# Packing the gate and up turns into one PSUM bank and one copy, and fusing two coefficient multiplies, in a fused state-space and ReGLU backward kernel

## The chip, the cores and the metric

One core of a Trainium2 chip. The metric is the device time of one execution in microseconds (us).

The engines are called PE (TensorE, matmuls and transposes), ACT (ScalarE), DVE (VectorE), POOL (GpSimd) and SP (SyncE, issues DMAs). PSUM is where PE writes; ACT and DVE move ("evict") its results into SBUF.

## The reference

The forward pass is a layernorm whose result feeds two branches that are added to the input: a state-space convolution (done by FFT) and a feed-forward block. The kernel computes the output and the gradients of all inputs.

```python
gate = x @ W_gate;  up = x @ W_up           # x: 2048 x 576, weights 576 x 4608
gate = gate * (gate > 0)
h    = gate * up
y    = h @ W_down                           # 4608 x 576
# convolution branch: K[d,l] = Re sum_n C[d,n] exp(l*dt*A[d,n]) dt*B[d,n],  y_A = fft_conv(u, K) + u*Dskip
# out = x0 + y_A(xn) + y_B(xn);  then jax.vjp: gradients of 12 inputs
```

## The kernel before

The feed-forward block runs in 12 chunks of 384 hidden columns. For each chunk, each of its three tiles of 128 columns and each of four groups of 512 rows (144 units in all), a unit computes gate, up and the gradient of h (15 matmuls of 128x512), makes three tiles T (h, and the gradients of gate and up), and *turns* them: PE transposes each into PSUM, and an engine copies the result into hN, dgN or duN, which the weight gradients of the chunk read later. The convolution's work (named S4 in the code, tiles ps_s) is woven in between by generators.

```python
def copy(self, out, in_, cols, scale=None, fp32=True):      # class Balance: who evicts?
    cd = cols * (1.09e-3 if fp32 else 0.56e-3) + 0.06       # account of DVE
    ca = cols * 0.84e-3 + 0.06                              # account of ACT
    if self.d + cd <= self.a + ca:  ...  # DVE copies
    else:                           ...  # ACT copies

# a_unit, for gate, up and dh in turn:
    for k in range(NK):
        nc.tensor.matmul(ps[:], lhsT=w[:, k, fs], rhs=rhs[:, k, :], ...)
    for _ in turns:
        next(src)                                           # one turn: 4 transposes, one copy

def t_steps(self, units):
    for c, sg, ft in units:
        for src, dst in zip(self.T[(c, sg, ft)], (self.hN, self.dgN, self.duN)):
            pt = g.psum_mm.tile([P, 512], F32, name="ps_mm")[:].bitcast(BF16)...   # 5 buffers of a bank
            for j in range(JS):                                                    # JS = 4
                nc.tensor.transpose(out=pt[:, j, :], in_=src[:, j * P:(j + 1) * P], ...)
            g.bal.copy(dst[...], pt[:, 0:JS, :], 512, fp32=False)                  # half a bank
            yield

# p2, generation of the convolution kernel, 36 groups of 16 channels:
    v.tensor_tensor(xa[:], pw[:, 1, hs]..., self.ev[:]..., op=ALU.mult)            # starts a group
    ...                                                                            # cut
    v.tensor_tensor(X[:, :, 0:2, :], Wv..., ex..., op=ALU.mult)
    nc.scalar.activation(X[:, :, 2, :], X[:, :, 0, :], ACT.Copy, scale=-1.0)
    v.tensor_tensor(w1, pw[:, 2, hs]..., X[:, :, 1:3, :]..., op=ALU.mult)          # w1 lies in tile xa
    v.tensor_tensor(w2, pw[:, 3, hs]..., X[:, :, 0:2, :]..., op=ALU.mult)          # w2 lies in tile W
    v.tensor_tensor(XC[:]..., w1, w2, op=ALU.subtract)
    ...                                  # cut: Y, V by group of 4; matmuls; sums(): V = X * psum, reduced
```

## Time and profile before

| | before |
|---|---|
| median of the first three runs | 1794.33 us |
| PE / DVE / ACT busy | 96% / 74% / 66% |
| PE starts later than its own spacing (gaps over 60 ns, at full clock) | 103 us |
| the same, lost at half clock | 10 us |

The first two lines are from the page: the span, and each engine's busy time, its share and its instructions.

```profile
span 1792.3 us, 42070 instructions
...
PE 1719.7 (96%) x16449; PEld 1184.7 (66%) x16449; DVE 1317.8 (74%) x2867; ACT 1189.2 (66%) x2736; POOL 205.0 (11%) x246
```

The next lines are the view of stretches (from:to in us, its length, busy us and instructions of PE, weight loads, DVE, ACT, POOL, then granted clock, DMA share and GB/s).

```profile
core 0: us, PE busy (x) PEld busy (x) DVE busy (x) ACT busy (x) POOL busy (x), PEclk, DMA share, GB/s
...
100.00:290.00 190.00, 170.70 (x1358) 109.97 (x1357) 139.38 (x322) 133.40 (x326) 16.02 (x21) 0.97 0.96 306
290.00:1490.00 1200.00, 1174.09 (x11904) 818.03 (x11903) 961.86 (x1956) 817.11 (x1838) 160.23 (x168) 1.00 0.70 183
```

In the long middle stretch PE is busy 98% of the time, DVE 80% and ACT 68%.

The last two rows of the table are not on the page. I take the start of each matmul and of the next: in this trace matmuls that follow each other stand 216 ns apart for 512 columns, 162 for 384, 122 for 288, 62 for 144 and 56 for 128 (medians), which N/2.4 + 2.5 ns for N columns fits, and 25 ns for 16 and 32. What a pair has beyond that is PE's wait. The view of groups, ACT only, shows the evictions (line, engine, op, tiles, sizes, count | busy us, mean ns of one | idle us before them and what ended it):

```profile
L68 ACT CAST osx<-ps_mm 128x288 bf16<-128x288 f32 x682 | 260.5, 428 | 50.5 <-PE ps_mm L298 47.6
...
L68 ACT COPY dgN<-ps_mm 128x512 bf16<-128x512 bf16 x140 | 83.8, 599 | 17.3 <-PE ps_mm L270 16.3
L68 ACT CAST dhb<-ps_mm 128x512 bf16<-128x512 f32 x141 | 83.8, 594 | 49.6 <-PE ps_mm L244 47.7 <-DVE dhb L221 0.8
L68 ACT COPY duN<-ps_mm 128x512 bf16<-128x512 bf16 x135 | 81.9, 607 | 1.5 <-PE ps_mm L270 1.1
L68 ACT COPY hN<-ps_mm 128x512 bf16<-128x512 bf16 x137 | 81.6, 595 | 1.2 <-PE ps_mm L270 1.2
```

The turn copies cost about 0.60 us each. The two multiplies, DVE's groups:

```profile
L867 DVE TENSOR_TENSOR xa<-pw,X 128x512 f32<-128x512 f32 x36 | 24.5, 681 | 0.1
L868 DVE TENSOR_TENSOR W<-pw,X 128x512 f32<-128x512 f32 x36 | 24.5, 681 | 0.0
```

### The profile page before, as it was taken

To read this page: it belongs to the slowest core of one execution; us is meant where nothing else is said; L and a number is where in the kernel's file an instruction comes from. 1 tells how busy PE (TensorE), PEld (TensorE's weight loads), DVE (VectorE), ACT (ScalarE), POOL (GpSimd) and SP (SyncE) were. 2 spreads that over 40 slices of the span, in tenths; PEclk is the share of its full clock that TensorE was granted. 3 is DMA by queue.
4 is the path that set the end of the run, shared out by engine and by line. 5 is a ranking of instruction groups with operands and counts; after the bars stand their busy time and mean duration, and the time that the engine had idled before them with its cause. 6 is when DMAs were issued, how large, how long until landed. Compare 5 with 4: busy or idle time off the path is not lost.

```text
span 1792.3 us, 42070 instructions
## 1 busy us (share of the span) xinstructions
PE 1719.7 (96%) x16449; PEld 1184.7 (66%) x16449; DVE 1317.8 (74%) x2867; ACT 1189.2 (66%) x2736; POOL 205.0 (11%) x246
## 2 busy tenths in 40 slices
PE   7989989999999999999999999999999998999998
PEld 5665557667667666766766766766676675676776
DVE  7575884677789788678787889889978962972551
ACT  5875874786688477568468658747857845864651
POOL 0200112011022011012101101101111100110000
PEclk9999999999999999999999999999999999999999
DMA  9799989679568656766858856866766578995873
GB/s 297 265 332 303 331 233 295 194 182 253 165 145 228 192 139 157 226 183 147 229 154 190 230 156 142 212 188 151 181 185 152 112 212 257 260 288 157 270 240 100
DMA packets 239004, 373.30 MB, mean 208 GB/s; under 512 B 49491, under 2 KB 153429, under 8 KB 237269
## 3 DMA queue, kind: packets, MB, share of 16 engines
q1 hardware_dynamic: 212836, 304.09, 52.4%
q0 software_dynamic: 24384, 51.92, 18.6%
q10 hardware_dynamic: 1584, 14.60, 2.3%
q8 instruction: 129, 2.11, 0.5%
q14 instruction: 71, 0.57, 0.1%
HBM read 233.10 MB, written 137.43 MB: 207 GB/s over the span
## 4 chain that ended last, share of the span: by engine, by line
PE 63%; DVE 21%; ACT 7%; DMA 6%; issue 3%; SPq 1%; POOL 0%; ACTq 0%; DVEq 0%; POOLq 0%
PE ps_mm L298 17%; PE ps_mm L244 15%; PE ps_mm L352 11%; PE ps_mm L336 6%; PE ps_mm L270 3%; DVE V L935 2%; DVE T L261 2%; DVE Sm L936 2%; DVE V L881 1%; DVE Y L882 1%; DVE Y L880 1%; DVE rg L254 1%; PE ps_mm L370 1%; DMA gT<-in_gT_dram 1%; DVE X L861 1%
## 5 line engine op out<-in xcount | busy, mean ns | idle before, releaser
L298 PE MATMUL ps_mm<-wf,T 128*128 128x288 bf16 x3456 | 481.8, 287 | 7.4 <-DVE T L256 2.6
L298 PEld LDWEIGHTS <-T 128*128 128x128 bf16 x3456 | 324.5, 98 | 97.0 <-issue 12.9
L68 ACT CAST osx<-ps_mm 128x288 bf16<-128x288 f32 x682 | 260.5, 428 | 50.5 <-PE ps_mm L298 47.6
L311 POOL DMA_DIRECT2D acc_dram<-osx x160 | 138.8, 867 | 1027.8 <-ACT osx L68 590.7
L352 PEld LDWEIGHTS <-rows 128*128 128x128 bf16 x1536 | 146.2, 98 | 95.4 <-issue 1.6
L244 PE MATMUL ps_mm<-xT,wd_150 128*128 128x512 bf16 x720 | 181.1, 379 | 4.1 <-ACT xT L153 1.6
L270 PEld LDWEIGHTS <-T 128*128 128x128 bf16 x1728 | 127.5, 98 | 86.3 <-issue 4.7
L244 PE MATMUL ps_mm<-xT,wd_151 128*128 128x512 bf16 x720 | 180.8, 380 | 0.0
L254 DVE SCALAR_TENSOR_TENSOR rg<-rg,ps_mm 128x512 bf16<-128x512 bf16 x144 | 98.2, 682 | 108.3 <-PE ps_mm L244 68.6
L244 PE MATMUL ps_mm<-gT,wd_152 128*128 128x512 bf16 x705 | 175.9, 379 | 0.7 <-DMA gT<-in_gT_dram 0.7
L270 PE MATMUL ps_mm<-ident_bf,T 128*128 128x128 bf16 x1728 | 157.6, 220 | 4.8 <-DVE T L256 1.9
L336 PE MATMUL ps_mm<-rows,hN 128*128 128x144 bf16 x2304 | 158.9, 227 | 0.0
L336 PEld LDWEIGHTS <-hN 128*128 128x128 bf16 x2304 | 148.5, 98 | 8.0 <-issue 5.4
L68 ACT CAST obw<-ps_mm 128x384 bf16<-128x384 f32 x103 | 49.2, 478 | 144.7 <-PE ps_mm L352 112.4
L352 PE MATMUL ps_mm<-dgN,rows 128*128 128x384 bf16 x768 | 136.8, 326 | 0.5 <-DMA rows<-xs_dram_141 0.5
L352 PE MATMUL ps_mm<-duN,rows 128*128 128x384 bf16 x768 | 135.6, 326 | 0.0
L253 ACT ACTIVATE rg<-ps_mm 128x512 bf16<-128x512 f32 x144 | 86.9, 603 | 52.1 <-PE ps_mm L244 51.5
L68 ACT CAST dhb<-ps_mm 128x512 bf16<-128x512 f32 x141 | 83.8, 594 | 49.6 <-PE ps_mm L244 47.7
L261 DVE TENSOR_TENSOR T<-dhb,rg 128x1024 bf16<-128x1024 bf16 x141 | 101.0, 717 | 19.4 <-ACT dhb L68 18.7
L244 PEld LDWEIGHTS <-wd_150 128*128 128x128 bf16 x720 | 66.0, 97 | 61.5 <-issue 3.7
L244 PEld LDWEIGHTS <-wd_151 128*128 128x128 bf16 x720 | 65.4, 98 | 59.9 <-issue 3.3
L244 PEld LDWEIGHTS <-wd_152 128*128 128x128 bf16 x705 | 63.4, 98 | 58.8 <-issue 1.8
(2506 smaller groups left out, 3042.2 us busy)
## 6 DMA issues: line engine op xcount, KB each, us to landing
acc_dram<-osx POOLq DMA_DIRECT2D x176, 288.0 KB, 5.1
gT<-in_gT_dram SPq DMA_DIRECT2D x48, 640.0 KB, 6.2
xT<-xT_dram SPq DMA_DIRECT2D x44, 640.0 KB, 5.8
rows<-in_gq_dram SPq DMA_DIRECT2D x48, 576.0 KB, 4.3
wf<-in_Wf_dram ACTq DMA_DIRECT2D x11, 1296.0 KB, 8.9
ex_dram<-exs SPq DMA_DIRECT2D x36, 320.0 KB, 4.6
ex<-ex_dram SPq DMA_DIRECT2D x36, 320.0 KB, 4.5
out_dram<-obw SPq DMA_DIRECT2D x96, 96.0 KB, 2.7
```

What stands on the lines that cost most here:

```text
L68: self.nc.scalar.copy(out, in_)
L244: nc.tensor.matmul(ps[:], lhsT=w[:, k, fs], rhs=rhs[:, k, :], start=(k == 0), stop=(k == NK - 1))
L253: nc.scalar.activation(rg, ps_g[:], ACT.Relu)
L254: nc.vector.scalar_tensor_tensor(upm, rg, 0.0, ps_u[:], op0=ALU.is_gt, op1=ALU.mult)
L261: nc.vector.tensor_tensor(T[:, 1:3], dhb.unsqueeze(1).to_broadcast([P, 2, JS * P]), ru[:], op=ALU.mult)
L270: nc.tensor.transpose(out=pt[:, j, :], in_=src[:, j * P:(j + 1) * P], identity=g.ident_bf[:])
L298: nc.tensor.matmul(ps[:, cs], lhsT=lt, rhs=rh, start=(i == 0), stop=(i == len(mms) - 1))
L311: nc.gpsimd.dma_start(g.acc_dram[:, t, :, :], o[:], accum_op=ALU.add)
L336: nc.tensor.matmul(ps[:, ft * 144:(ft + 1) * 144], lhsT=self.hN[:, st, ft * P:(ft + 1) * P], rhs=gq[:, st, :], start=(st == 0), stop=(st = ...
L352: nc.tensor.matmul(ps[:, :Fc], lhsT=xs[:, st, 0:P], rhs=src[:, st, :], start=(st == 0), stop=(st == ST - 1))
L935: nc.vector.tensor_tensor(pr[:, vi], X[:, dx:dx + DG, r0:r0 + 2].rearrange("p d r a -> p d (r a)").unsqueeze(2).to_broadcast(sh), psg[:, 0 ...
L936: nc.vector.tensor_reduce(out=Sm[:, :, s0 + dd:s0 + dd + DG, :].rearrange("p v d j -> p v (d j)"), in_=pr.rearrange("p v d j c -> p v (d j ...
```

## The change

Intent: fewer fixed costs on ACT and DVE, and fewer PSUM tiles. The turns of the two gradients share a bank, eight transposes of 128x128 bf16, and leave it in one copy of 1024 columns; the two multiplies become one over both planes (which needs the planes of `pw` swapped, and an input that reads overlapping windows of X).

```diff
-        self.dgN = wp.tile([P, ST, Fc], BF16, name="dgN")
-        self.duN = wp.tile([P, ST, Fc], BF16, name="duN")
+        self.gN = wp.tile([P, 2, ST, Fc], BF16, name="gN")
+        self.dgN, self.duN = self.gN[:, 0], self.gN[:, 1]
 ...                                                            # a_unit: 2 turns per unit, behind up and dh
-            for _ in turns:
+            n = (2 * len(turns) * (i + 1)) // 3 - (2 * len(turns) * i) // 3
+            for _ in range(n):
                 next(src)
 ...                                                            # t_steps
-            for src, dst in zip(self.T[(c, sg, ft)], (self.hN, self.dgN, self.duN)):
+            for which in ((0,), (1, 2)):
+                n = len(which) * JS
                 pt = g.psum_mm.tile([P, 512], F32, name="ps_mm")...
-                    nc.tensor.transpose(out=pt[:, j, :], in_=src[:, j * P:(j + 1) * P], ...)
-                g.bal.copy(dst[...], pt[:, 0:JS, :], 512, fp32=False)
+                for i, w in enumerate(which):
+                    for j in range(JS):
+                        nc.tensor.transpose(out=pt[:, i * JS + j, :], in_=src[w][:, j * P:(j + 1) * P], ...)
+                if n == JS:
+                    g.bal.copy(self.hN[:, js, fs], pt[:, 0:n, :], n * P, fp32=False)
+                else:
+                    g.bal.copy(self.gN[:, :, js, fs], pt[:, 0:n, :].rearrange(...), n * P, fp32=False)
 ...                                                            # p2
-                w1 = xp.tile(xs, F32, name="xa")...
-                w2 = xp.tile([P, 2, SX, NE], F32, name="W")...
-                v.tensor_tensor(w1, pw[:, 2, hs]..., X[:, :, 1:3, :]..., op=ALU.mult)
-                v.tensor_tensor(w2, pw[:, 3, hs]..., X[:, :, 0:2, :]..., op=ALU.mult)
-                v.tensor_tensor(XC[:]..., w1, w2, op=ALU.subtract)
+                w = xp.tile([P, 2, SX, NE], F32, name="W")...
+                xv = bass.AP(x.tensor, x.offset, [x.ap[0], (16, 2)] + list(x.ap[1:]))
+                v.tensor_tensor(w, pw[:, 2:4, hs]..., xv, op=ALU.mult)
+                v.tensor_tensor(XC[:]..., w[:, 1], w[:, 0], op=ALU.subtract)
```

More of the change, by code (lines that the diff above doesn't have):

```diff
@@ L245, in a_unit @@
             pss.append(ps)
-            for _ in turns:
+            n = (2 * len(turns) * (i + 1)) // 3 - (2 * len(turns) * i) // 3
+            for _ in range(n):
                 next(src)
-            yield NK * 0.2158 + len(turns) * 0.22
+            yield NK * 0.2158 + n * 0.33
         ps_g, ps_u = pss[0:2]
@@ L266, in t_steps @@
         for c, sg, ft in units:
-            for src, dst in zip(self.T[(c, sg, ft)], (self.hN, self.dgN, self.duN)):
+            src, js, fs = self.T[(c, sg, ft)], slice(sg * JS, (sg + 1) * JS), slice(ft * P, (ft + 1) * P)
+            for which in ((0,), (1, 2)):
+                n = len(which) * JS
                 pt = g.psum_mm.tile([P, 512], F32, name="ps_mm")[:].bitcast(BF16).rearrange("p (k t) -> p k t", t=P)
-                for j in range(JS):
-                    nc.tensor.transpose(out=pt[:, j, :], in_=src[:, j * P:(j + 1) * P], identity=g.ident_bf[:])
-                g.bal.copy(dst[:, sg * JS:(sg + 1) * JS, ft * P:(ft + 1) * P], pt[:, 0:JS, :], 512, fp32=False)
+                for i, w in enumerate(which):
+                    for j in range(JS):
+                        nc.tensor.transpose(out=pt[:, i * JS + j, :], in_=src[w][:, j * P:(j + 1) * P], identity=g.ident_bf[:])
+                if n == JS:
+                    g.bal.copy(self.hN[:, js, fs], pt[:, 0:n, :], n * P, fp32=False)
+                else:
+                    g.bal.copy(self.gN[:, :, js, fs], pt[:, 0:n, :].rearrange("p (i j) t -> p i j t", i=2), n * P, fp32=False)
                 yield
@@ L599, in params @@
                 v.tensor_tensor(p1[:], p1[:], p2[:], op=op)
-                v.tensor_tensor(pw[:, 2 + j, :], p1[:], dt[:], op=ALU.mult)
+                v.tensor_tensor(pw[:, 3 - j, :], p1[:], dt[:], op=ALU.mult)
                 bal.add(d=2.6)
@@ L863, in p2 @@
                 XC = xop.tile([P, SX, 2, 16], BF16, name="XC")
-                xw = [P, SX, 32]
-                w1 = xp.tile(xs, F32, name="xa")[:].rearrange("p d e -> p (d e)")[:, 0:SX * 32].rearrange("p (d e) -> p d e", e=32)
-                w2 = xp.tile([P, 2, SX, NE], F32, name="W")[:].rearrange("p r d e -> p (r d e)")[:, 0:SX * 32].rearrange("p (d e) -> p d e", e=32)
-                v.tensor_tensor(w1, pw[:, 2, hs].unsqueeze(2).to_broadcast(xw), X[:, :, 1:3, :].rearrange("p d r a -> p d (r a)"), op=ALU.mult)
-                v.tensor_tensor(w2, pw[:, 3, hs].unsqueeze(2).to_broadcast(xw), X[:, :, 0:2, :].rearrange("p d r a -> p d (r a)"), op=ALU.mult)
-                v.tensor_tensor(XC[:].rearrange("p d r a -> p d (r a)"), w1, w2, op=ALU.subtract)
+                xw = [P, 2, SX, 32]
+                w = xp.tile([P, 2, SX, NE], F32, name="W")[:].rearrange("p r d e -> p (r d e)")[:, 0:2 * SX * 32].rearrange("p (w d e) -> p w d e", w=2, e=32)
+                x = X[:, :, 0:2, :].rearrange("p d r a -> p d (r a)")
+                xv = bass.AP(x.tensor, x.offset, [x.ap[0], (16, 2)] + list(x.ap[1:]))
+                v.tensor_tensor(w, pw[:, 2:4, hs].unsqueeze(3).to_broadcast(xw), xv, op=ALU.mult)
+                v.tensor_tensor(XC[:].rearrange("p d r a -> p d (r a)"), w[:, 1], w[:, 0], op=ALU.subtract)
                 bal.add(d=6.5, a=2.5)
@@ L952, in param_grads @@
         S_r, S_i, T_r, T_i = Sm[:, 0, :, 0], Sm[:, 1, :, 0], Sm[:, 0, :, 1], Sm[:, 1, :, 1]
-        pA, pB, cr, ci = (pw[:, i, hs] for i in range(4))
+        pA, pB, ci, cr = (pw[:, i, hs] for i in range(4))
         ob = lambda: yop.tile([P, DG, 2, P], BF16, name="Y")[:].rearrange("p d r q -> p (d r q)")[:, 0:DH]
```

## The prediction

> **What bounds the kernel now.** TensorE. The page's busy table gives PE 1719.7 us of 1792.3 (96%), VectorE (DVE) 1317.8 (74%), ScalarE (ACT) 1189.2 (66%). The timeline shows that PE runs at its own spacing nearly all the time: ten 128x512 matmuls take 2.16 us, eighteen 128x288 take 2.21, sixteen 128x384 take 2.60. From consecutive matmul starts I count about 100 us in which PE issued later than that spacing (gaps over 60 ns), plus about 10 us lost in five stretches at half the clock (granted clock 0.97 in 100-290 us). The Trainium skill, "TensorE: Matmul & The Clock Gate", Part 1, says that an idle window of about 3.4 us halves the clock; the trace agrees: after a 2.4 us wait near 643 us 128x512 matmuls stand 0.43 us apart instead of 0.216. Of the 100 us, about 30 follow an ACT result and 25 a DVE result; others are start-up, DMA round trips or unknown.
>
> **What the change does.** (a) The matmuls and the transposes keep their number and, as the instruction orders of the two builds show, almost exactly their order. PE's own floor doesn't move. (b) 432 evictions of 128x512 bf16 become 144 of 128x512 and 144 of 128x1024; the build gives 136 of the large ones to ACT, 8 to DVE (before: ACT 412, DVE 20). By the group table an ACT copy of 512 takes 0.600 us, one of 1024 (YT, same shape) 1.02, so the busy sum of ACT falls by about 25 us. But instructions overlap: back to back, starts are 0.477 us apart for 512 and 0.909 for 1024, so ACT's queue really gains only 2 x 0.477 - 0.909 = 0.045 us a pair, about 6.5 us in all. The skill, "ScalarE: Activation LUTs", says the same (a fixed term of 186 ns, of which about 93 ns overlap). (c) Two 128x512 fp32 multiplies (0.681 us each, 0.602 apart) become one of 1024; estimate 1.21 us, 1.135 apart: 36 x 0.07 = 2.5 us of DVE queue, about 5 us of its busy sum. (d) A unit takes two turn tiles in place of three from the five-buffer PSUM pool, so reuse is less tight; against that a bank stays closed for 0.9 us in place of 0.48, and evictions behind the long copy wait up to 0.4 us longer.
>
> **How much is on the critical path.** The chain of waits is 63% PE, 21% DVE, 7% ACT. Relief of 1-2% in ACT's queue and 0.3% in DVE's shortens only those of PE's waits that are an eviction late: about 50 us of waits, of which I expect 3 to 8 us to go, and the long copies to give 1 to 3 back. Order changes on ACT and DVE add some chance of either sign, above all whether one of the half-clock stretches appears or goes.
>
> **Prediction.** 1789 us (before 1794.33), range 1779 to 1799 (8 in 10). Chances: faster by over 2% 0.02, within 2% 0.97, slower 0.01.
>
> **What would show it.** ACT busy about 1165 us, DVE about 1310, PE unchanged within 6 us; 144 copies into gN of about 1.03 us on ACT; the multiply about 1.2 us x36; waits of PE that follow ACT somewhat smaller; DMA unchanged.
>
> **What would make it wrong.** If PSUM reuse (d) was the real cause of many small PE waits, the gain could reach 15-20 us. If the long copies hold up the convolution's evictions, or the multiply's overlapping read is slow (over 1.5 us), it could be slower by 5-10 us.

The trace does not quite agree with the idle window of 3.4 us that the prediction takes from the skill: the clock records of the kernel before show half clock from 643.8 us, after a single wait of 2.26 us (2.4 us by the starts of the matmuls), and none after two other waits of 2.26 us (to 239.6 and 272.4 us); the half-clock stretch at 715.5 us follows three waits of 0.76, 0.59 and 0.26 us. The measured stretches decide. And the gain of 0.045 us a pair is the measured one alone, not the skill's (see the last section).

## More of the kernel before

The order in which DVE and ACT get their instructions is not that of the source: it is settled when the program is built, and the traces show it.

From 100 to 290 us the DMA engines are busy 96%, and PE 90%.

## The result, and the profile after

| | before | after |
|---|---|---|
| median, runs of the same rounds | 1794.96 us (4 runs) | 1798.58 us (4 runs) |
| ratio | | 1.0015, 95% interval 0.9997 to 1.0032 |
| the same in five further rounds | 1795.29 us (11 runs) | 1798.06 us (6 runs) |
| ratio there | | 1.0016, interval 1.0001 to 1.0031 |

Ratios are the mean time of one kernel's runs over that of the other's of the same rounds, so not quite the ratio of the medians. The change won nothing, and the second set places it just on the slow side, by some 3 us.

The page of the kernel after, then its stretches (same columns as above):

```profile
span 1797.1 us, 41897 instructions
...
PE 1719.4 (96%) x16449; PEld 1183.1 (66%) x16449; DVE 1313.0 (73%) x2821; ACT 1176.0 (65%) x2602; POOL 204.2 (11%) x246
```

```profile
100.00:290.00 190.00, 168.66 (x1303) 106.73 (x1301) 138.71 (x317) 131.70 (x313) 15.07 (x20) 0.96 0.94 298
290.00:1490.00 1200.00, 1171.35 (x11936) 817.79 (x11934) 958.16 (x1920) 806.58 (x1741) 160.40 (x169) 1.00 0.70 183
```

PE's busy time is unchanged to 0.3 us. ACT gave up 13 us and DVE 5, as intended, and PE did not use them. The evictions and the one multiply after:

```profile
L68 ACT CAST osx<-ps_mm 128x288 bf16<-128x288 f32 x681 | 256.0, 435 | 47.4 <-PE ps_mm L305 45.7
L68 ACT COPY gN<-ps_mm 128x1024 bf16<-128x1024 bf16 x136 | 140.1, 1030 | 8.8 <-PE ps_mm L274 8.5
...
L68 ACT COPY hN<-ps_mm 128x512 bf16<-128x512 bf16 x141 | 83.6, 593 | 26.1 <-PE ps_mm L274 26.0
L68 ACT CAST dhb<-ps_mm 128x512 bf16<-128x512 f32 x141 | 83.4, 591 | 51.2 <-PE ps_mm L244 48.0 <-DVE dhb L221 1.3
```

```profile
L875 DVE TENSOR_TENSOR W<-pw,X 128x1024 f32<-128x1024 f32 x36 | 43.8, 1217 | 0.0
```

Each operation came out as costed: 1.030 us for a copy of 1024, 1.217 us for the multiply. Of the ACT time saved, part became idle time: before its turn copies (hN and gN) ACT now sits idle 34.9 us in all, nearly all of it waiting for PE's transposes (20.0 us before hN, dgN and duN in the kernel before). The Trainium skill, "ScalarE: Activation LUTs", § What ACT_TABLE_LOAD costs, gives 186 ns + 0.833 ns a column for an ACTIVATE with immediate scale and bias. An estimate from that for 512 and 1024 columns is 612 and 1039 ns, and the copies of this trace agree (593 to 607 and 1030 ns).

**Where the time lies.** PE executes the feed-forward matmuls in the same order in both programs (10,337 of them without the turns' transposes), so the k-th matmul of one trace can be set against the k-th of the other. The lag of this matmul, in us, read where the kernel before stands at the time given:

| lag against the one trace of before, us | at 145 | at 290 | at 1490 | at 1785 |
|---|---|---|---|---|
| after | 2.5 | 3.7 | 4.7 | 4.9 |
| after, a second trace | 0.8 | 0.7 | 2.0 | 1.0 |

From 290 us on, where most of the changed instructions are, the change is worth +1.2 or +0.3 us: nothing. The two traces of one kernel differ by 4 us, most of it collected before 290 us. So a systematic difference, if any, is of the size of what one execution differs from the next.

**PE's waits by what ended them** (same counting as in the table of before; us):

| | after an ACT result | after a DVE result | of these, the V product beyond 290 us | all |
|---|---|---|---|---|
| before | 36.4 | 27.6 | 5.3 | 103.4 |
| after | 33.3 | 36.0 | 8.7 | 109.6 |
| after, second trace | 31.1 | 34.5 | 8.7 | 105.2 |

The waits for ACT did shrink by 3 to 5 us. Those for DVE grew by 7 to 8. Two places show how. The timelines below have start us, us, engine, line, op, tiles and sizes, and in brackets the idle time before it and its releaser.

*First place, near 135 us.* Before:

```profile
133.24 0.82 DVE L585 TENSOR_TENSOR exs<-pw,ev 128x640 f32<-128x640 f32 x1 [5.89 <-DMA ex_dram<-exs]
...
134.50 0.45 DVE L62 CAST fA_2069<-ps_s_2070 128x288 bf16<-128x288 f32 x1
...
134.87 0.45 DVE L62 CAST fA_2069<-ps_s_2096 128x288 bf16<-128x288 f32 x1
135.00 0.28 PE L628 MATMUL ps_s_2099<-sig,Sx 128*128 128x288 bf16 x1 [3.15 <-DVE fA_2069 L62]
```

and after:

```profile
137.82 0.82 DVE L592 TENSOR_TENSOR exs<-pw,ev 128x640 f32<-128x640 f32 x1 [6.54 <-DMA ex_dram<-exs]
138.56 0.45 DVE L62 CAST fA_2098<-ps_s_2102 128x288 bf16<-128x288 f32 x1
...
138.93 0.45 DVE L62 CAST fA_2098<-ps_s_2122 128x288 bf16<-128x288 f32 x1
139.06 0.40 PE L635 MATMUL ps_s_2130<-sig,Sx 128*128 128x288 bf16 x1 [5.67 <-DVE fA_2098 L62]
```

In both, DVE stands at a multiply that needs an `exs` buffer whose store has not landed. Evictions of finished matmuls (fA) stand behind it in DVE's queue, and PE runs out of PSUM buffers. The Trainium skill, "TensorE: Matmul & The Clock Gate", Part 1, calls the queues of ACT and DVE strict FIFO; that is what is seen. PE waits 3.15 us before and 5.67 us after: DVE was released by the store at 133.2 us in one and at 137.8 us in the other. By the traces' clock records PE ran at half clock around the end of this wait, for 3.4 us before and for 6.8 us after (in the second trace of the change for 3.4 us, with a wait of 5.3 us).

*Second place, near 1140 us.* Before:

```profile
1140.59 0.69 DVE L859 TENSOR_TENSOR B<-W,ex 128x512 bf16<-128x512 f32 x1
...
1141.19 0.74 DVE L935 TENSOR_TENSOR V<-X,ps_s_18919 128x256 f32<-128x256 f32 x2
...
1141.99 0.62 PE L917 MATMUL ps_s_18963<-ident_bf,Y 128*128 128x128 bf16 x8 [0.31 <-DVE V L935]
```

and after:

```profile
1143.43 0.69 DVE L866 TENSOR_TENSOR B<-W,ex 128x512 bf16<-128x512 f32 x1
...
1144.04 0.82 DVE L851 TENSOR_TENSOR xa<-pw,ev 128x640 f32<-128x640 f32 x1
1144.77 0.74 DVE L942 TENSOR_TENSOR V<-X,ps_s_18678 128x256 f32<-128x256 f32 x2
...
1145.57 0.62 PE L924 MATMUL ps_s_18716<-ident_bf,Y 128*128 128x128 bf16 x8 [1.77 <-DVE V L942]
```

Here V, the product that frees the PSUM buffer PE wants, has the first multiply of the *next* group (`xa`, 0.82 us) in front of it in DVE's order. Before, the V product came directly behind B. PE's wait grew from 0.31 to 1.77 us. In the traces, the next of the ops xa, V, Y and XC behind this `xa` is such a V product 22 times of 36 before and 27 times after.

### The profile page after: what moved, and what is told of

Same layout as the page of the kernel before. It is cut to its first block, busy times and chain, and to the rows that moved or that the text cites. A ratio compares the mean times of both kernels' runs of the same rounds, so it can differ in the third digit from the quotient of the medians.

```text
span 1797.1 us, 41897 instructions
## 1 busy us (share of the span) xinstructions
PE 1719.4 (96%) x16449; PEld 1183.1 (66%) x16449; DVE 1313.0 (73%) x2821; ACT 1176.0 (65%) x2602; POOL 204.2 (11%) x246
## 5 line engine op out<-in xcount | busy, mean ns | idle before, releaser
L305 PEld LDWEIGHTS <-T 128*128 128x128 bf16 x3456 | 324.5, 98 | 100.3 <-issue 16.7
L68 ACT CAST osx<-ps_mm 128x288 bf16<-128x288 f32 x681 | 256.0, 435 | 47.4 <-PE ps_mm L305 45.7
L359 PE MATMUL ps_mm<-gN,rows 128*128 128x384 bf16 x1536 | 265.2, 326 | 0.0
L274 PEld LDWEIGHTS <-T 128*128 128x128 bf16 x1728 | 119.5, 98 | 58.5 <-DVE T L262 0.7
L68 ACT COPY gN<-ps_mm 128x1024 bf16<-128x1024 bf16 x136 | 140.1, 1030 | 8.8 <-PE ps_mm L274 8.5
L274 PE MATMUL ps_mm<-ident_bf,T 128*128 128x128 bf16 x1728 | 141.1, 220 | 0.3 <-DVE T L262 0.2
```

The costliest lines, as they stand in the source:

```text
L68: self.nc.scalar.copy(out, in_)
L274: nc.tensor.transpose(out=pt[:, i * JS + j, :], in_=src[w][:, j * P:(j + 1) * P], identity=g.ident_bf[:])
L305: nc.tensor.matmul(ps[:, cs], lhsT=lt, rhs=rh, start=(i == 0), stop=(i == len(mms) - 1))
L359: nc.tensor.matmul(ps[:, :Fc], lhsT=xs[:, st, 0:P], rhs=src[:, st, :], start=(st == 0), stop=(st == ST - 1))
```

## The experiments

Twelve runs, all with five rounds; each row is against the runs of before. Kernels are compared only within the same rounds. Every interval lies within 1% of 1. "Lag" is that of the table above, from each run's single trace, and has the 4 us of scatter seen there; the three calls also ran on three different chips.

| run | median, us | ratio to before (95%) | lag at 145 / 290 / 1490 / 1785 us |
|---|---|---|---|
| after_again | 1798.06 | 1.0016 (1.0001 to 1.0031) | 0.8 / 0.7 / 2.0 / 1.0 |
| only_turns | 1801.49 | 1.0041 (1.0026 to 1.0055) | 3.2 / 5.0 / 8.2 / 7.5 |
| only_multiply | 1797.62 | 1.0015 (0.9994 to 1.0035) | 0.9 / 2.2 / 6.4 / 5.9 |
| pair_in_two_copies | 1795.83 | 1.0007 (0.9991 to 1.0022) | -1.0 / 0.2 / 4.4 / 6.1 |
| before_act_only | 1801.81 | 1.0033 (1.0021 to 1.0045) | -1.0 / 8.4 / 7.8 / 9.0 |
| after_act_only | 1799.26 | 1.0028 (1.0015 to 1.0042) | 0.0 / 2.7 / 4.6 / 5.1 |
| thin_turns (wrong result) | 1795.06 | 0.9997 (0.9985 to 1.0009) | -0.4 / 4.4 / 3.1 / 2.7 |
| no_multiply (wrong result) | 1801.92 | 1.0033 (1.0021 to 1.0045) | 1.3 / 0.3 / 4.9 / 4.7 |
| before_late_act_only | 1794.28 | 0.9995 (0.9981 to 1.0008) | -3.1 / 4.1 / 4.4 / 3.7 |
| after_late_act_only | 1800.72 | 1.0023 (1.0008 to 1.0038) | -4.8 / 2.9 / 6.2 / 6.8 |
| before_negate_on_dve | 1798.07 | 1.0018 (1.0001 to 1.0035) | -0.8 / 2.3 / 6.4 / 5.3 |
| after_negate_on_dve | 1806.82 | 1.0063 (1.0051 to 1.0075) | 2.8 / 5.3 / 12.8 / 14.3 |

### The change and its parts

after_again is the change unaltered. only_turns keeps the two multiplies, only_multiply keeps the three turn copies. pair_in_two_copies is the change with

```diff
-                    g.bal.copy(self.gN[:, :, js, fs], pt[:, 0:n, :].rearrange(...), n * P, fp32=False)
+                    for i in range(2):
+                        g.bal.copy(self.gN[:, i, js, fs], pt[:, i * JS:(i + 1) * JS, :], JS * P, fp32=False)
```

> The changed kernel once more, unaltered, in five rounds, so that its parts can be compared with it on one chip. Theory A (eviction relief is off the critical path; the only systematic loss lies before 290 us, where DVE waits for the exs stores and holds evictions behind it): 1.000 to 1.003 of before, with the lag of the matmuls behind those of before built up before 290 us and flat afterwards. Theory B (the shorter queue does win several us, and the longer copies give them back by holding up other evictions): the same total, but the lag moves up and down by several us after 290 us.

> The merged turns alone, the two multiplies as before. Theory A: the same time as the whole change within 2 us, and 0 to 5 us over before, with the extra in 100 to 290 us. Theory B: over before by 3 us or more, spread over the whole span, since the long copies are all here and the multiply's gain is missing.

> The one multiply for both planes alone, the turns as before. Its 36 ops free about 2.5 us of DVE's queue, all after 290 us, and the 100 to 290 us stretch is that of before. Theory A: within 2 us of before. Theory B says the multiply is pure gain: 1 to 3 us faster than before.

> The whole change, but the bank filled by gate and up leaves in two copies of 512 instead of one of 1024: order of TensorE and bank use are those of the change, the long copy is gone. Theory A: the same as the change within 2 us, although the busy sum of ACT rises by about 20 us. Theory B: 2 to 6 us faster than the change, since no eviction waits behind a copy of 1 us; if instead the saved fixed cost matters, 3 to 6 us slower.

The whole change repeated at 1.0016, and its lag before 290 us was only 0.7 us this time, so "built up before 290 us" does not hold for each execution. The multiply alone gave no gain (1.0015, median 2.3 us over before), against theory B, and just beyond the 2 us of theory A. Its trace has the new DVE waits: 8.8 us for V beyond 290 us, against 5.3 us in before and in only_turns. The turns alone came out at 1.0041, 6 us over before, outside what theory A expected and *slower than the whole change*. Theory B's numbers for this run fit (3 us or more, spread over the span: the lag is 3.2, 5.0, 8.2 and 7.5 us), but its gain from the multiply did not come. The parts don't add up, and I can't say why this one build is slow. Taking the long copy away leaves the time where it was within the noise (1.0007, interval overlapping that of the change, medians 2.2 us apart). By the six runs of each, that copy costs 1.8 us, with an interval from -1 to +5 us: that long copies hold up other evictions is neither shown nor excluded.

The wait near 139 us is 5.5 us in after_again and 5.4 us in only_turns, but 2.6 us in only_multiply and 2.7 us in pair_in_two_copies (by the distance of matmul starts; 3.3 us in before, 5.8 us in after). So it follows the build with one long copy, and repeats. The next runs ask whether it costs what it lasts.

### How much is relief of ACT or DVE worth at all?

thin_turns is the kernel before with the turn copies of all chunks but the first cut to 16 of 128 columns, the account of Balance unchanged, so that each engine keeps its copies. The order did not stay quite the same, as the expectation assumed: the build moved 96 of DVE's 2867 instructions and 64 of ACT's 2736 (those outside the longest order that both traces share; two traces of the same kernel have no such difference). Three outputs (the weight gradients) are wrong.

```diff
-    g.bal.copy(dst[:, ..., ft * P:(ft + 1) * P], pt[:, 0:JS, :], 512, fp32=False)
+    w = P if c == 0 else 16
+    g.bal.copy(dst[:, ..., ft * P:ft * P + w], pt[:, 0:JS, 0:w], 512, fp32=False)
```

> Wrong result on purpose: from the second chunk on, each of the three turn copies of a unit carries 16 of its 128 columns, so 396 evictions of 0.6 us shrink to about 0.2 and ACT's queue loses about 140 us, some twenty times what the change can win. Order, bank use and all other instructions are those of the kernel before. Theory A (eviction throughput is not what TensorE waits for): 0 to 12 us faster than before, that is under a tenth of the work taken away. Theory D (each us of ACT's queue is worth a fair share of a us): 30 us or more faster.

Its page, its stretch from 290 us, and ACT's groups:

```profile
span 1795.0 us, 42075 instructions
...
PE 1720.6 (96%) x16449; PEld 1185.0 (66%) x16449; DVE 1316.2 (73%) x2867; ACT 1066.6 (59%) x2736; POOL 203.8 (11%) x246
```

```profile
290.00:1490.00 1200.00, 1171.52 (x11951) 819.75 (x11949) 961.37 (x1954) 726.60 (x1841) 159.80 (x170) 1.00 0.70 184
```

```profile
L68 ACT CAST osx<-ps_mm 128x288 bf16<-128x288 f32 x682 | 259.4, 411 | 81.0 <-PE ps_mm L299 77.6
...
L68 ACT CAST dhb<-ps_mm 128x512 bf16<-128x512 f32 x141 | 82.9, 588 | 78.5 <-PE ps_mm L244 77.1 <-DVE dhb L221 0.6
...
L68 ACT COPY dgN<-ps_mm 128x64 bf16<-128x64 bf16 x130 | 28.3, 218 | 30.2 <-PE ps_mm L270 30.1
```

ACT is busy 123 us less, nine times the relief of the change, and the kernel is no faster (0.9997). The time went into ACT's own waiting: 81.0 us idle before the osx evictions instead of 50.5, 78.5 us before dhb instead of 49.6, ended by PE in nearly all of it. ACT empties its queue sooner and then waits for PE's next result. PE's waits that follow an ACT result are 33.0 us in this trace, against 36.4 us in before: nearly all of them were there for another reason than ACT's load. Theory D, which asked for 30 us, falls for ACT; the moved order could hide some gain, but among the correct builds, whose orders differ more, none is more than 12 us slower than before. So theory A's first half holds for ACT to within about a tenth of the work taken away.

no_multiply leaves both multiplies out of the kernel before. Its outputs 0 and 1 are wrong.

```diff
-    v.tensor_tensor(w1, ...); v.tensor_tensor(w2, ...); v.tensor_tensor(XC[:]..., w1, w2, op=ALU.subtract)
+    v.tensor_tensor(XC[:]..., XC_in[:, :, 16:48], XC_in[:, :, 0:32], op=ALU.subtract)   # XC_in: X itself
```

> Wrong result on purpose: both coefficient multiplies are left out of the kernel before, the subtraction reads the powers directly. DVE loses 72 ops, about 43 us of its queue, seventeen times what the one multiply of the change wins. Theory A: 0 to 8 us faster than before, so that the part of the change is worth under 0.5 us. Theory D: 15 us or more faster.

```profile
span 1796.9 us, 42012 instructions
...
PE 1723.9 (96%) x16449; PEld 1187.2 (66%) x16449; DVE 1278.1 (71%) x2795; ACT 1188.6 (66%) x2736; POOL 204.8 (11%) x246
```

```profile
290.00:1490.00 1200.00, 1171.73 (x11883) 817.23 (x11881) 921.07 (x1880) 814.45 (x1834) 159.77 (x168) 1.00 0.69 182
```

DVE is busy 40 us less, and the kernel is *slower*, by 1.0033. Neither theory expected that; theory D falls for DVE too. This edit moves DVE's order more than the thin copies do (277 of the 2795 instructions that are left, by the same count), and the place near 1140 us looks as it does in the change (timeline of no_multiply):

```profile
1140.80 0.82 DVE L844 TENSOR_TENSOR xa<-pw,ev 128x640 f32<-128x640 f32 x1
...
1141.54 0.74 DVE L931 TENSOR_TENSOR V<-X,ps_s 128x256 f32<-128x256 f32 x2
...
1142.34 0.62 PE L913 MATMUL ps_s<-ident_bf,Y 128*128 128x128 bf16 x8 [1.51 <-DVE V L931]
```

Again `xa` of the next group stands before V, and PE waits 1.51 us. Tile `xa` is not used by the multiplies in any of the kernels that leave w1 out; that this lets the build place the next group's first op earlier is my reading of the code, not a test of its own. The waits for V beyond 290 us are 8.6 to 8.8 us in six of the seven traces with the one multiply and 7.2 us in no_multiply. The seventh, after_negate_on_dve, has 7.3 us. With two multiplies they are 5.3 to 5.5 us in four of six traces, 6.2 us in thin_turns and 7.1 us in before_negate_on_dve. So the order of a build moves these waits by 1 to 2 us even where the multiplies stay.

### Taking the waits away one by one

act_only sends all balanced evictions to ACT while the convolution's first transform runs, so that none can stand behind the `exs` wait on DVE; late_act_only does so only in the second half of it, and carries no debt of the account over. Both were run on both kernels.

```diff
-        if self.d + cd <= self.a + ca:
+        if self.d + cd <= self.a + ca and not self.act_only:
 # act_only: act_only = True through the transform of half 0
 # late_act_only: from its 9th of 16 steps; at its end  g.bal.a = g.bal.d + debt
```

> The kernel before, with every balanced eviction given to ACT while the first transform of half 0 runs (about 95 to 145 us), so that none stands in DVE's queue behind the multiply that waits for an exs store. Theory A (the systematic extra of the change is the longer wait of TensorE near 139 us, 5.4 to 5.8 us in three traces with merged turns, 2.6 to 3.3 in three without): the 3.3 us wait near 135 us goes, and with it some of the half-clock time behind it: 2 to 6 us faster than before. Theory C (the waits there belong to the full DMA queues and only move): within 1.5 us of before.

> The same edit in the changed kernel. Theory A: the 5.4 to 5.8 us wait goes; 4 to 9 us faster than the change, and the change then costs nothing: within 1.5 us of the kernel before with the same edit. Theory B (long copies hold up evictions everywhere): still 2 us or more behind the kernel before with the same edit.

> The kernel before; balanced evictions go to ACT only in the second half of the first transform (about 120 to 145 us, 11 evictions moved), and no debt is carried over to DVE afterwards. Theory A (an eviction behind DVE's exs wait costs its wait in time): the wait of 3.3 us near 135 us goes and nothing takes its place, 2 to 4 us faster than before. Theory C (in this stretch, where the DMA engines are over 90% busy, a wait that is taken away comes back at the next transfer): within 1.5 us.

> The same edit in the changed kernel. Theory A: its wait of 5.4 to 5.8 us near 139 us goes, 4 to 7 us faster than the change, level with the edited kernel before within 1.5 us. Theory C: within 1.5 us of the change, 1 to 4 us over before.

act_only did remove the wait near 135 us, and was slower in the kernel before (1.0033): ACT, now alone, held PE up between 104 and 110 us, and DVE, to which the account then gave the next evictions, held it up for 4.0 us at 166 us. In the changed kernel (1.0028) the same edit took the wait near 139 us away and brought one of 4.0 us at 167 us; it was no faster than the change, against theory A, and not behind the edited kernel before (1799.26 and 1801.81 us), against theory B. That edit was too blunt. late_act_only is the cleaner one. Against the trace of before it is ahead at 145 us by 3.1 us (edited kernel before) and by 4.8 us (edited change), so about the wait that was taken away or a little more. At 290 us it is *behind* that trace by 4.1 and 2.9 us. What took its place, in the edited kernel before:

```profile
160.14 0.83 DVE L586 TENSOR_TENSOR exs<-pw,ev 128x640 f32<-128x640 f32 x1 [0.70 <-DMA ex_dram<-exs]
...
162.11 0.70 ACT L69 CAST s_ug<-ps_s 128x288 bf16<-128x288 f32 x2
...
162.56 0.45 PE L650 MATMUL ps_s<-b_ug,FM 128*64 128x288 bf16 x2 [3.63 <-ACT s_ug L69]
```

Some 27 us after the place of the old wait, ACT stands behind the same kind of multiply for `exs`, held by the same stores, and PE waits 3.63 us there, against 1.08 us in the kernel before. The edited change has a wait of 3.3 us at 161 us, where the change has none. The totals are 0.9995 and 1.0023. Both fit theory C: in this stretch, with the DMA engines over 90% busy, the wait of PE that was taken away came back some 20 to 30 us later. For the changed kernel theory A is out, which asked for 4 to 7 us less than the change and the level of the edited kernel before, and with it my reading that the change's lag is the 2.5 us by which one of its waits is longer. For the kernel before alone it is not quite out: the interval (0.9981 to 1.0008) leaves room for a gain of up to 3 us.

negate_on_dve moves one op of ACT, behind which evictions stand, to DVE. In the kernel before, ACT waited for DVE's X, an eviction (fC) stood behind, and PE waited for that eviction:

```profile
641.08 0.68 DVE L861 TENSOR_TENSOR X<-W,ex 128x512 f32<-128x512 f32 x1
...
641.79 0.42 ACT L862 ACTIVATE X<-X 128x256 f32<-128x256 f32 x1 [3.04 <-DVE X L861]
...
642.39 0.40 ACT L68 CAST fC_10464<-ps_s_10465 128x288 bf16<-128x288 f32 x1
...
642.85 0.35 PE L907 MATMUL ps_s_10499<-XC,Y 128*128 128x16 bf16 x8 [2.26 <-ACT fC_10464 L68]
```

```diff
-    nc.scalar.activation(X[:, :, 2, :], X[:, :, 0, :], ACT.Copy, scale=-1.0)
+    v.tensor_scalar(X[:, :, 2, :], X[:, :, 0, :], -1.0, None, op0=ALU.mult)
```

> The kernel before, but the negated third plane of the powers is made by DVE right after the powers, not by ACT, where evictions stand behind that op while it waits for DVE (23 us in 22 waits; the wait of TensorE near 643 us is one of them). Theory E (what TensorE waits for is the place in the queues, not their load): the 2.4 us wait near 643 us and some others go although DVE gets 36 ops more: 3 to 8 us faster. Theory A in its narrow form (latencies that no local edit moves): within 2 us.

> The same edit in the changed kernel, so that both parts of the change run with it. Theory E: 3 to 8 us faster than the change, and at or below the kernel before. Theory A in its narrow form: within 2 us of the change.

The wait near 643 us went, in both. In its place, ten microseconds on (edited kernel before):

```profile
653.34 3.47 PE L298 MATMUL ps_mm<-wf,T 128*128 128x288 bf16 x27 [1.82 <-DVE rg L254]
...
659.72 0.31 PE L645 MATMUL ps_s<-b_ug,FM 128*64 128x288 bf16 x2 [1.66 <-ACT s_ug L68]
```

two waits of 1.82 and 1.66 us. Neither kernel got faster (1.0018 and 1.0063); the second is the slowest, 7.5 us of its lag collected between 290 and 1490 us, with 39.4 us of waits after DVE results against 36.0 in the change. Theory E, that a better place in the queue wins the wait's length, fell with this edit: it removed the wait it aimed at, and others came. Theory A's narrow form, within 2 us, was missed as well: the medians are 3.0 us over before and 8.8 us over the change. No run beats the kernel before by more than the scatter.

## Why the prediction was right or wrong

- **The range and the chances held.** 1798.58 us lies in 1779 to 1799, but only 0.4 us from its end, less than what one execution differs from the next: that it fell inside is luck. The change is within 2%. The centre, 1789, was about 10 us low, and the direction it gave, 5 us faster, did not come.
- **What bounds the kernel: right.** PE at 96%, unchanged to 0.3 us, with some 100 us of waits that the change could at most have shortened.
- **The costs of operations: right.** 136 large copies on ACT at 1.030 us (predicted about 1.03; the "144" in the list of signs counted DVE's 8 too), the multiply at 1.217 us (1.2), both spacings as worked out: starts are 0.904 us apart for back-to-back copies of 1024 (0.909 predicted) and 1.135 us for the multiply (1.135). DVE busy 1313.0 (about 1310). ACT busy was put at 1165 and measured 1176.0: I took the sum of the durations (25 us less), but the page counts overlapping instructions once, so the fall is 13 us.
- **The step that failed** is the term "about 50 us of waits, of which I expect 3 to 8 us to go, and the long copies to give 1 to 3 back". The ACT side did shrink by 3 to 5 us. But 7 to 8 us came up behind DVE, and the trace beyond 290 us ends +0.3 or +1.2 us. The term assumed that a wait ended by an engine is shorter when that engine has less to do. thin_turns speaks against it for ACT: 123 us of work less, nothing gained (0.9985 to 1.0009), 33.0 us of waits after ACT results left of 36.4.
- **"Order changes on ACT and DVE add some chance of either sign" was probably the part that mattered**, and was given no number. Builds that differ in a few instructions lie between 0.9995 and 1.0063.
- **PSUM reuse (d)** was named as what could make the gain 15 to 20 us. With fewer tiles (the change, only_turns) and where banks are held shorter still (thin_turns) nothing is gained, so no such cause showed. The other fear, a slow overlapping read, did not come true either.
- **Open:** how much of the 3 us is the change itself. Seen is that six of seven one-multiply builds have about 3 us more of waits for V than most two-multiply builds; that these make the 3 us, and that the freed tile makes the waits, is not tested. Not settled is why only_turns is slower than the whole change, and how much of the lag before 290 us is chance from run to run.

## What to carry to other kernels

When one engine is busy 96% and the others 66 to 74%, count the waits of that engine and ask for each whether a lighter queue or an earlier place in the queue would end it; here a lighter ACT queue was worth nothing that could be measured, even at nine times the relief of the change. An experiment that thins the work and moves as little else as it can (copy fewer columns, wrong result accepted) estimates the ceiling of such a change in one run, before it is built; check in the trace what it did to the order all the same. Fusing two ops may also free a tile, and with it let the build move other ops ahead of one that somebody waits for, so compare the order on each engine for the ops that release PSUM.

## What the Trainium skill lacked or had wrong

- "ScalarE: Activation LUTs", § What ACT_TABLE_LOAD costs: back-to-back ACTIVATEs are said to overlap by about 93 ns. Copies out of PSUM overlap by 120 to 126 ns here (0.600 us long and 0.477 apart; 1.030 long and 0.904 apart), so merging two copies of 512 wins only 0.05 us, where an estimate from the page's figures gives 0.09.
- "VectorE: DVE Perf Modes", § Rules for kernel authors, advises "Minimize op *count*, not sems". Here 36 ops fewer gave 1.0015 of the time and 72 ops fewer 1.0033: where PE, not DVE, is 96% busy the count alone won nothing. What the row lacks is the order that a build gives DVE's ops, which moved with the count.
- "TensorE: Matmul & The Clock Gate", Part 1, has the strict order of ACT's and DVE's queues as a line on queue depths. What follows from it here, an op that waits for a DMA holding finished evictions behind it until PE stops (3.2 to 5.7 us of PE's time near 135 us, and 3.4 to 6.8 us at half clock, in the traces of before and of the change), is not on that page.
